# Agent attention and a feed-forward layer: where the query probabilities are split into two float32r parts

## The chip, the cores and the metric

The kernel runs on one core of a Trainium2 chip. The metric is the device time of one launch in microseconds; the kernel before took 1161.85 us, the median of three runs (1158.37 to 1161.86).

## The reference

Two layers follow each other. With q, k, v of shape (2, 12480, 128) and 49 agent vectors per batch:

```python
a2k = sm(agents, k)        # softmax over 12480 keys
agent_v = a2k @ v
q2a = sm(q, agents)        # softmax over 49 agents, one row per query
x = q2a @ agent_v
h = x @ w_in               # 128 -> 2048
g = where(h > 0, h, exp(min(h, 0)) - 1)
out = g @ w_out            # 2048 -> 128
```

All is float32 (the weights arrive as float64 and are converted on the chip).

## The kernel before, in words

The product `agent_v @ w_in` is formed once per batch as the table A (49 rows, 2048 columns), so that h is the query probabilities times A. A query block has 960 queries; there are 26 (13 for each batch). One block runs through 16 steps of the main loop: two halves of 480 query columns, eight steps each, and each step covers 256 of the 2048 hidden columns. A step s does, in this order: the score-side products `p1` (L397 to L406) into one of three PSUM tiles `h` of two banks, the output products `p2` of step s - 4 (L426 to L450) into two PSUM banks `o0` and `o1` that are held for eight steps, the activation `elu` (ACT Relu and Exp, L411 and L414, then DVE's combination into `g`, L416), and `split` (DVE casts half of `g` to `hi`, L422; GpSimd subtracts to get `lo`). When a half of a block ends, both output banks are evicted: `ob` by DVE (L442) and `oa` by ACT between its Relu and Exp (L446); GpSimd adds the two, and the next half's `p2` can write into the banks.

Products of float32 accuracy are made of two float32r parts, high and low: A has `ahi` and `alo`, w_out has `w_hi` and `w_lo` for one half of the hidden columns, and the query probabilities have `px0`, `px1`. The other half of w_out is `w_f`, a plain float32 tile, against which plain float32 `g` is multiplied.

The query probabilities of block j are made while block j - 1 is computed. `manual_schedule` keeps the order in which the program is written, and `at(s, fn, ...)` (L456) puts a piece of work behind step s; pieces at the same step stand in the order in which they were added. Scores, row maximum and subtraction come first; then the exponential on ACT (`q_exp`, one step on), the row sums and a small operation that adds 1e-9 (`q_sum`, `q_rz(0)`, L326), the reciprocal and the normalisation in place (`q_rz(1)`, `q_mul`, L333), the cast to the high part on ACT (`q_hi`, L338, a helper at L193), and the low part on DVE (`q_lo`, L342, a helper at L198). Their tiles `pp_hi` and `pp_lo` hold 120 queries in the partitions and four pairs of 49 probabilities in columns 0 to 48 and 64 to 112. `q_ring` (L362) takes one `h` tile, turns both parts with TensorE's transpose (L355, eight in all), has DVE copy each bank to `px` (L358), and sends `px` by DMA on SP's queue to `py` with the two halves of the partitions exchanged (L359, L360).

Block 0 is made in a prologue (L459 to L606), which also takes the key statistics of batch 0, and in which weight chunks are converted by DVE, ACT and GpSimd. `plan` (L560 on) lists its order row by row, and rows 8 to 22 have extra matmuls `busy(6)` behind them that only occupy TensorE. While the first half of the main loop runs, the key scores of batch 1 are computed in it as well (two rounds per block, `k_round`); in the middle, its weighted sums (`ev1`).

Of the kernel before, what the change touches and what calls it, by code (L numbers as in the profile page):

```python
# [8 lines left out]
F32 = mybir.dt.float32  # L9
F32R = mybir.dt.float32r  # L10
I32 = mybir.dt.int32
U32 = mybir.dt.uint32
ACTF = mybir.ActivationFunctionType
ALU = mybir.AluOpType
AX = mybir.AxisListType

TP = 120
R = 8
# [4 lines left out]
def tile_agent_attention_moe(  # L23
# [10 lines left out]
    nc = tc.nc  # L34
    B, C, N = kT.shape
    NA = agT.shape[2]
    ROWS = (0, 64)
    NA2 = ROWS[1] + NA
# [3 lines left out]
    T = G // 2  # L42
# [11 lines left out]
    const = ctx.enter_context(tc.tile_pool(name="const", bufs=1))  # L54
# [4 lines left out]
    sm_p = ctx.enter_context(tc.tile_pool(name="sm", bufs=2))  # L59
# [2 lines left out]

    ag_sb = const.tile([C, B, NA], F32)
    ident = const.tile([128, 128], F32)
    ident_r = const.tile([128, 128], F32R)
    dup = const.tile([NA, NA2], F32)
    ones = const.tile([NA, TP], F32)
    pp_hi = const.tile([TP, R // 2, NA2], F32R)
    pp_lo = const.tile([TP, R // 2, NA2], F32R)
    win_sb = big.tile([C, DFF], F32)  # L70
    w_f = big.tile([128, NP, 128], F32)
    w_hi = big.tile([128, NP, 128], F32R)
# [38 lines left out]
    k_t, v_t, q_t, p_t, A = {}, {}, {}, {}, {}  # L111
# [17 lines left out]
    idle = []  # L129
    held = {}  # L130

    def slot(dt=F32):

        return ps_h.tile([128, 2, 512], dt, tag="h", name="h")
# [36 lines left out]
    def k_max_t(run, ps):  # L171
        nc.tensor.transpose(ps[:NA, :TP], run, ident[:TP, :TP])
        mx_st["pt"] = ps

    def k_max_d(g):
        nc.vector.tensor_reduce(out=mcs[:, g:g + 1], in_=mx_st["pt"][:NA, :TP], axis=AX.X, op=ALU.max)
        attn_free(mx_st.pop("pt"))
        dg = sm_p.tile([NA, NA], F32, tag="dg", name="dg")
        nc.vector.tensor_scalar(out=dg, in0=ident[:NA, :NA], scalar1=mcs[:, g:g + 1], scalar2=None, op0=ALU.mult)
        mx_st["dg"] = dg  # L180
# [10 lines left out]
    def cast_hi(eng, out, x):  # L191
        if eng is nc.scalar:
            nc.scalar.activation(out=out, in_=x, func=ACTF.Copy)  # L193
        else:
            eng.tensor_scalar(out=out, in0=x, scalar1=1.0, scalar2=0.0, op0=ALU.mult, op1=ALU.add)

    def rest(eng, out, x, hi):
        eng.tensor_tensor(out=out, in0=x, in1=hi.bitcast(F32), op=ALU.subtract)  # L198
# [94 lines left out]
    q_st = {}  # L293
# [29 lines left out]
    def q_rz(half):  # L323
        z = q_st["z"]
        if half == 0:
            nc.vector.tensor_scalar(out=z, in0=z, scalar1=1e-9, scalar2=None, op0=ALU.add)  # L326
        else:
            q_st["z"] = sm_p.tile([TP, R], F32, tag="z", name="z")
            nc.vector.reciprocal(out=q_st["z"], in_=z)

    def q_mul(eng):
        e = q_st["e"]
        eng.tensor_tensor(out=e, in0=e, in1=q_st["z"].unsqueeze(2).to_broadcast([TP, R, NA]), op=ALU.mult)  # L333

    def halves(t):
        return [t[:, :, r:r + NA] for r in ROWS]

    def q_hi(eng):  # L338
        for h, t in enumerate(halves(pp_hi)):
            cast_hi(eng, t, q_st["e"][:, h * (R // 2):(h + 1) * (R // 2), :])  # L340

    def q_lo(eng, lo=0, hi=R):  # L342
        for x in range(lo, hi, R // 2):
            h = x // (R // 2)
            rest(eng, halves(pp_lo)[h], q_st["e"][:, x:x + R // 2, :], halves(pp_hi)[h])

    def q_tr(j, banks):

        p_t[j] = []
        for part, (src, ps) in enumerate(zip((pp_hi, pp_lo), banks)):  # L350
            x = sm_p.tile([NA2, T], F32R, tag=f"px{part}", name=f"px{part}")
            y = sm_p.tile([NA2, T], F32R, tag=f"py{part}", name=f"py{part}")
            p_t[j].append((x, y))
            for i in range(R // 2):
                nc.tensor.transpose(ps[:NA2, i * TP:(i + 1) * TP], src[:, i, :], ident_r[:TP, :TP])  # L355
        a, b = [slice(r, r + NA) for r in ROWS]
        for (x, y), ps in zip(p_t[j], banks):
            nc.vector.tensor_copy(out=x, in_=ps[:NA2, 0:T])  # L358
            nc.sync.dma_start(out=y[a].bitcast(F32), in_=x[b].bitcast(F32))  # L359
            nc.sync.dma_start(out=y[b].bitcast(F32), in_=x[a].bitcast(F32))  # L360

    def q_ring(j):  # L362
        t = slot(F32R)
        q_tr(j, [t[:, i, :] for i in range(2)])

    wr_t = {}

# [5 lines left out]
    def wo_step(c):  # L373

        if c not in wo_gen:
            even = wc_p.tile([128, 2, 128], F32, tag="even", name="even")
            w_e[c] = even
            pick = [lambda x, i=i: x.rearrange("p (m i d) -> p m i d", i=2, d=128)[:, :, i, :] for i in range(2)]
            wo_gen[c] = f64_steps(wr_t.pop(c), [(even, pick[0]), (w_f[:, 2 * c:2 * c + 2, :], pick[1])])
        next(wo_gen[c])  # L380
# [71 lines left out]
    act, dve, pool = nc.scalar, nc.vector, nc.gpsimd  # L452
# [3 lines left out]
    def at(s, fn, *a):  # L456
        pre.setdefault(s, []).append((fn, a))

    with tc.manual_schedule():  # L459
        with tc.tile_pool(name="pro", bufs=5) as pro, tc.tile_pool(name="ps_p", bufs=1, space=bass.MemoryType.PSUM) as ps_p:  # L460
# [5 lines left out]
            def win_step(c):  # L466
                if c not in win_gen:
                    win_gen[c] = f64_steps(win_r.pop(c), [(win_sb[:, c * 512:(c + 1) * 512], lambda x: x)])
                next(win_gen[c])
# [33 lines left out]
            dve.memset(ones, 1.0)  # L503
            dve.memset(s_all[:, :, R:R + 1, :], 0.0)
            dve.memset(ebias, -8.0 * 896 * 2 ** 20)
            dve.tensor_copy(out=ident_r, in_=ident)
            dve.memset(dup, 0.0)
            dve.memset(pp_hi.bitcast(F32), 0.0)
            dve.memset(pp_lo.bitcast(F32), 0.0)
            for r in ROWS:  # L510
                dve.tensor_copy(out=dup[:, r:r + NA], in_=ident[:NA, 0:NA])
            hk = ps_p.tile([128, 2, 512], F32, tag="hk", name="hk")
# [21 lines left out]
            for c, t in enumerate(CONV):  # L534
                f = [lambda c=c: win_step(c) if c < 4 else wo_step(c - 4)] * 7
                f = [f[0:2], f[2:4], f[4:6], f[6:7]]
# [5 lines left out]
            def conv():  # L542
                for x in ff.pop(0):
                    x()

            qq = [q_max, q_sub, q_exp, q_sum, lambda: q_rz(0), lambda: q_rz(1), lambda: q_mul(dve), lambda: q_hi(act), lambda: q_lo(dve)]

            def run(l, n=1):
                for _ in range(n):
                    l.pop(0)()  # L550

            def top(g):
                k_max_t(runs[g], hk[:, 0, :])
                k_max_d(g)

            def spread():
# [15 lines left out]
                ("s11", "p7", lambda: run(qq, 2)),  # L572
                ("e4", lambda: run(qq, 2)),
                ("s12", "p8", lambda: run(qq, 2)),
                ("e5", lambda: run(qq, 3)),
                (lambda: top(2), lambda: q_tr(0, [x.bitcast(F32R) for x in idle]), ev0_scale),
                ("e6", spread, "p9"),
                ("e7", "p10"),
                ("e8", "p11"),
# [39 lines left out]
        for j in range(1, B * NG):  # L619
            s0 = (j - 1) * NM + EDGE  # L620
            if j + 1 < B * NG:
                at(s0 + 1, load_q, j + 1)
            if j > 1:
                s0 -= NP
            at(s0 - 2 * (j == 1), q_scores, j, 0, R)
            at(s0 - 2 * (j == 1), q_max)
            at(s0 - 2 * (j == 1), q_sub)
            at(s0 + 1, q_exp)
            at(s0 + 2, q_sum)
            at(s0 + 2, q_rz, 0)  # L630
            at(s0 + 3, q_rz, 1)
            at(s0 + 3, q_mul, dve)
            at(s0 + 4, q_hi, act)
            at(s0 + 5, q_lo, dve, 0, 4)
            at(s0 + 6, q_lo, dve, 4, 8)
            at(s0 + (9 if j == 1 else NP + 4), q_ring, j)
        def k_round(r):
            ps = attn_bank()
# [3 lines left out]
        for r in range(NR):  # L642
            s0 = (r // 2) * NM + 13 + 4 * (r % 2)
# [8 lines left out]
        for r in range(NR):  # L652
            s0 = (7 + r // 3) * NM + 8 + 4 * (r % 3)
# [57 lines left out]
```

## Time and profile before

| | |
|---|---|
| median of three runs | 1161.85 us |
| lowest and highest run | 1158.37 and 1161.86 us |
| span of the profiled execution, first to last instruction | 1156.0 us |
| TensorE busy | 1122.3 us, 97% of the span |
| ACT busy | 898.3 us, 78% |
| DVE busy | 875.5 us, 76% |
| GpSimd busy | 599.8 us, 52% |
| 16 DMA engines | 58 GB/s on average |

The page gives the profiled execution's span and no other time of its own. A busy TensorE is not TensorE at its peak: matmuls are pipelined and their ends are modelled, so the time that one takes is best read from the start of one group to the start of the next. In the table, time in which an engine waits for a semaphore is not busy.

### The profile page before, as it was taken

Reading aid. Unit: us, or ns where it says so; the run is one execution under the profiler, and the core shown is the slowest. Engines: PE = TensorE matmul, PEld = TensorE weight load, DVE = VectorE, ACT = ScalarE, POOL = GpSimd, SP = SyncE. Lnnn points to the kernel's source line nnn. Section 1 sums busy time; section 2 is a strip of 40 time slices with the busy share of each in tenths; the row PEclk is TensorE's granted clock in tenths of the full one; section 3 lists DMA queues with packets and bytes.
Section 4 is the critical chain, followed back from the end, with each engine's and each line's share of the span. In section 5 each row is a group of like instructions: output and inputs, shape, how many; then the busy total and the mean of one; then the engine's idle time right before and its main releaser. Section 6 shows DMA issues by size and latency. Waiting matters only on the chain.

```text
span 1156.0 us, 21922 instructions
## 1 busy us (share of the span) xinstructions
PE 1122.3 (97%) x8364; PEld 871.2 (75%) x8364; DVE 875.5 (76%) x1313; ACT 898.3 (78%) x1050; POOL 599.8 (52%) x495
## 2 busy tenths in 40 slices
PE   9987999999999999999999999999999999999998
PEld 9974777777777777777776777777777777777787
DVE  5538777777777877777778877887788778877875
ACT  3217788788888878778778888888888888888896
POOL 0114555455555545545545555555555565655565
PEclk9999999999999999999999999999999999999999
DMA  9940121121121221221101101110111011101000
GB/s 297 256 139 1 40 82 44 40 82 56 33 77 57 69 74 57 69 75 57 35 24 40 35 23 49 39 35 23 48 40 35 23 48 37 38 23 48 19 23 18
DMA packets 25711, 66.66 MB, mean 58 GB/s; under 512 B 3054, under 2 KB 14806, under 8 KB 25606
## 3 DMA queue, kind: packets, MB, share of 16 engines
q1 hardware_dynamic: 25606, 65.26, 18.6%
q8 instruction: 66, 1.08, 0.4%
q14 instruction: 39, 0.32, 0.1%
HBM read 42.68 MB, written 12.78 MB: 48 GB/s over the span
## 4 chain that ended last, share of the span: by engine, by line
PE 76%; DVE 9%; ACT 4%; issue 2%; POOL 0%; DVEq 0%; POOLq 0%; ACTq 0%
PE o L437 45%; PE h L405 21%; PE h L150 6%; DVE g L416 6%; ACT e L411 2%; PE h L211 2%; PE h L355 2%; ACT e L414 1%; DVE hi L422 1%; DVE pp_lo L198 1%; DVE ob L442 1%; ACT pp_hi L193 1%; DVE qe L333 1%; PE h L264 0%; DVEq L422 0%
## 5 line engine op out<-in xcount | busy, mean ns | idle before, releaser
L198 POOL TENSOR_TENSOR lo<-g,hi 128x480 fp32r<-128x480 f32 x416 | 521.3, 1253 | 495.1 <-DVE hi L422 394.9
L416 DVE SCALAR_TENSOR_TENSOR g<-e,h 128x960 f32<-128x960 f32 x416 | 479.5, 1153 | 171.0 <-ACT e L414 168.5
L411 ACT ACTIVATE e<-h 128x960 f32<-128x960 f32 x416 | 401.6, 965 | 115.9 <-PE h L405 99.6
L414 ACT ACTIVATE e<-e 128x960 f32<-128x960 f32 x416 | 418.4, 1006 | 11.6
L437 PE MATMUL o<-g,w_f 64*128 64x480 f32 x1664 | 427.4, 562 | 0.0
L437 PE MATMUL o<-lo,w_hi 64*128 64x480 f32 x832 | 338.0, 751 | 0.0
L405 PE MATMUL h<-px,ahi 49*128 49x480 f32 x832 | 259.0, 391 | 4.6 <-DVE alo L286 3.9
L405 PE MATMUL h<-py,ahi 49*128 49x480 f32 x832 | 258.9, 391 | 0.5 <-DVE g L416 0.5
L422 DVE CAST hi<-g 128x480 fp32r<-128x480 f32 x416 | 179.5, 431 | 54.6 <-PE o L437 2.0
L437 PE MATMUL o<-hi,w_lo 64*128 64x480 f32 x832 | 189.4, 384 | 16.5 <-ACT oa L446 7.1
L437 PEld LDWEIGHTS o<-g,w_f 64*128 64x128 f32 x1664 | 181.7, 185 | 19.6
L437 PE MATMUL o<-hi,w_hi 64*128 64x480 f32 x832 | 184.4, 380 | 0.0
L405 PEld LDWEIGHTS h<-px,ahi 49*128 49x128 f32 x832 | 149.0, 187 | 41.0 <-issue 22.1
L405 PEld LDWEIGHTS h<-py,ahi 49*128 49x128 f32 x832 | 149.0, 187 | 38.3 <-issue 24.9
L405 PE MATMUL h<-py,alo 49*128 49x480 f32 x416 | 157.1, 378 | 0.0
L405 PE MATMUL h<-px,alo 49*128 49x480 f32 x416 | 157.0, 377 | 0.0
L437 PEld LDWEIGHTS o<-lo,w_hi 64*128 64x128 f32 x832 | 101.0, 186 | 67.1 <-issue 58.0
L437 PEld LDWEIGHTS o<-hi,w_lo 64*128 64x128 f32 x832 | 100.2, 185 | 41.2 <-ACT oa L446 17.3
L437 PEld LDWEIGHTS o<-hi,w_hi 64*128 64x128 f32 x832 | 99.2, 187 | 9.3
L405 PEld LDWEIGHTS h<-py,alo 49*128 49x128 f32 x416 | 77.0, 185 | 5.9
L405 PEld LDWEIGHTS h<-px,alo 49*128 49x128 f32 x416 | 77.1, 185 | 4.1
L447 POOL TENSOR_TENSOR ob<-ob,oa 128x480 f32<-128x480 f32 x52 | 63.3, 1217 | 3.9 <-ACT oa L446 3.9
(125 smaller groups left out, 794.7 us busy)
## 6 DMA issues: line engine op xcount, KB each, us to landing
v<-in_vx_dram SPq DMA_DIRECT2D x26, 483.8 KB
k<-in_kT_dram SPq DMA_DIRECT2D x26, 480.0 KB
q<-in_qT_dram SPq DMA_DIRECT2D x26, 480.0 KB
out_dram<-ob SPq DMA_DIRECT2D x52, 240.0 KB
py<-px SPq DMA_DIRECT2D x104, 91.9 KB
raw<-in_w_out_dram SPq DMA_DIRECT2D x4, 512.0 KB
raw<-in_w_in_dram SPq DMA_DIRECT2D x3, 512.0 KB
k<-in_w_in_dram SPq DMA_DIRECT2D x1, 512.0 KB
```

The source lines that it names most:

```text
L150: nc.tensor.matmul(out=ps[:TP, j * NA:(j + 1) * NA], lhsT=src[:, j * TP:(j + 1) * TP], rhs=ag_sb[:, b, :], start=True, stop=True)
L193: nc.scalar.activation(out=out, in_=x, func=ACTF.Copy)
L198: eng.tensor_tensor(out=out, in0=x, in1=hi.bitcast(F32), op=ALU.subtract)
L211: nc.tensor.matmul(out=ps, lhsT=s_all[:, r, j:j + 2, :].rearrange("p t a -> p (t a)"), rhs=v_t[b, r][:, j, :], start=(r == rs[0] and j == ...
L355: nc.tensor.transpose(ps[:NA2, i * TP:(i + 1) * TP], src[:, i, :], ident_r[:TP, :TP])
L405: nc.tensor.matmul(out=h[:, u, 0:T], lhsT=a[x, :], rhs=p[u ^ half][x, :], start=i == 0, stop=i == 2)
L411: nc.scalar.activation(out=e, in_=h, func=ACTF.Relu, scale=-1.0)
L414: nc.scalar.activation(out=e, in_=e, func=ACTF.Exp, scale=-1.0)
L416: nc.vector.scalar_tensor_tensor(out=g, in0=e, scalar=-1.0, in1=h, op0=ALU.add, op1=ALU.max)
L422: nc.vector.tensor_copy(out=hi_t[s], in_=g_t[s][:, 0, :])
L437: nc.tensor.matmul(out=o_t[u][:, 0:T], lhsT=w[x, c, :], rhs=v[x, :], start=first and i == 0, stop=last and i == len(jobs) - 1)
L447: nc.gpsimd.tensor_tensor(out=ob, in0=ob, in1=oa, op=ALU.add)
```

## The change

The normalisation writes its product to one float32 tile `pp` in place of `e`, and there is no split in front of the transposes. Four float32 transposes write to one bank; ACT copies the bank to the high part `px0` (rounding to float32r), and DVE subtracts this from the bank to get the low part `px1`. The exchanges by DMA stand behind each part as before. `q_mul` stands one step later than it did, and `q_hi` and `q_lo` with their places at steps 4, 5 and 6 are gone.

```diff
-    ident_r = const.tile([128, 128], F32R)
-    pp_hi = const.tile([TP, R // 2, NA2], F32R)
-    pp_lo = const.tile([TP, R // 2, NA2], F32R)
+    pp = const.tile([TP, R // 2, 128], F32)
...
+    def q_mul():
+        e = q_st["e"].rearrange("p (h i) a -> p h i a", h=2)
+        z = q_st["z"].rearrange("p (h i) -> p h i", h=2).unsqueeze(3).to_broadcast([TP, 2, R // 2, NA])
+        out = pp.rearrange("p i (h a) -> p h i a", h=2)[:, :, :, 0:NA]
+        nc.vector.tensor_tensor(out=out, in0=e, in1=z, op=ALU.mult)
+
+    def q_tr(ps):
+        for i in range(R // 2):
+            nc.tensor.transpose(ps[:NA2, i * TP:(i + 1) * TP], pp[:, i, 0:NA2], ident[:TP, :TP])
+        q_st["tr"] = ps[:NA2, 0:T]
+
+    def q_parts(j, part):
+        ps = q_st["tr"]
+        if part == 0:
+            p_t[j] = []
+        x = sm_p.tile([NA2, T], F32R, tag=f"px{part}", name=f"px{part}")
+        y = sm_p.tile([NA2, T], F32R, tag=f"py{part}", name=f"py{part}")
+        p_t[j].append((x, y))
+        if part == 0:
+            nc.scalar.activation(out=x, in_=ps, func=ACTF.Copy)
+        else:
+            rest(nc.vector, x, q_st.pop("tr"), p_t[j][0][0])
         a, b = [slice(r, r + NA) for r in ROWS]
+        nc.sync.dma_start(out=y[a].bitcast(F32), in_=x[b].bitcast(F32))
+        nc.sync.dma_start(out=y[b].bitcast(F32), in_=x[a].bitcast(F32))
...
     def q_ring(j):
-        t = slot(F32R)
-        q_tr(j, [t[:, i, :] for i in range(2)])
+        q_tr(slot()[:, 0, :])
+        q_parts(j, 0)
+        q_parts(j, 1)
...
-            dve.tensor_copy(out=ident_r, in_=ident)
-            dve.memset(pp_hi.bitcast(F32), 0.0)
-            dve.memset(pp_lo.bitcast(F32), 0.0)
+            dve.memset(pp, 0.0)
...
-                ("e5", lambda: run(qq, 3)),
-                (lambda: top(2), lambda: q_tr(0, [x.bitcast(F32R) for x in idle]), ev0_scale),
+                ("e5", lambda: run(qq, 1)),
+                (lambda: top(2), lambda: q_tr(idle[0]), lambda: q_parts(0, 0), lambda: q_parts(0, 1), ev0_scale),
...
             at(s0 + 3, q_rz, 1)
-            at(s0 + 3, q_mul, dve)
-            at(s0 + 4, q_hi, act)
-            at(s0 + 5, q_lo, dve, 0, 4)
-            at(s0 + 6, q_lo, dve, 4, 8)
+            at(s0 + 4, q_mul)
             at(s0 + (9 if j == 1 else NP + 4), q_ring, j)
```

## Rows read from the trace of the kernel before

**Rows 1.** Busy time by stretch: length, then each engine's busy us (instructions), clock, DMA

```profile
200.00:400.00 200.00, 199.49 (x1503) 152.89 (x1500) 158.33 (x236) 164.46 (x189) 106.95 (x88) 1.00 0.19 57
800.00:1000.00 200.00, 194.52 (x1448) 146.20 (x1446) 160.15 (x228) 168.15 (x192) 114.91 (x93) 1.00 0.11 35
```

**Rows 2.** Waits of TensorE, 620 to 1156 us: total us, times, longest

```profile
PE o L437 <- ACT oa L446: 7.1, 12, 0.6
PE o L437 <- DVE ob L442: 6.0, 12, 0.5
```

**Rows 3.** Timeline at one such wait: start, us, engine, line, operation, [idle before, releaser]

```profile
725.60 0.63 ACT L193 ACTIVATE pp_hi<-qe 120x196 fp32r<-120x196 f32 x2 [1.42 <-DVE qe L333]
...
731.87 0.38 PE L405 MATMUL h<-px,ahi 49*128 49x480 f32 x1
...
732.68 0.56 ACT L446 ACTIVATE oa<-o 128x480 f32<-128x480 f32 x1
...
733.29 0.48 PE L437 MATMUL o<-hi,w_lo 64*128 64x480 f32 x1 [0.60 <-ACT oa L446]
...
735.62 0.38 PE L405 MATMUL h<-px,ahi 49*128 49x480 f32 x1
```

**Rows 4.** Timeline, the same step of an earlier pass and the step before it

```profile
187.30 0.38 PE L405 MATMUL h<-py,ahi 49*128 49x480 f32 x1
...
188.17 0.39 PE L437 MATMUL o<-hi,w_hi 64*128 64x480 f32 x2
...
188.39 0.97 PE L437 MATMUL o<-g,w_f 64*128 64x480 f32 x4
...
188.82 0.76 PE L437 MATMUL o<-lo,w_hi 64*128 64x480 f32 x2
...
189.41 0.38 PE L405 MATMUL h<-px,ahi 49*128 49x480 f32 x1
...
191.79 0.38 PE L405 MATMUL h<-px,ahi 49*128 49x480 f32 x1
```

**Rows 5.** Timeline of TensorE at the eight transposes of block 1

```profile
128.11 0.61 PE L355 MATMUL h<-ident_r,pp_hi 120*113 120x120 f32 x4
128.55 0.56 PE L355 MATMUL h<-ident_r,pp_lo 120*113 120x120 f32 x4
129.04 0.49 PE L405 MATMUL h<-py,ahi 49*128 49x480 f32 x1
```

**Rows 6.** Line 172: count, duration ns minimum/median/maximum, first and last start

```profile
L172 PE MATMUL hk<-ident,mrun x3: 268/268/268, 17.3 to 59.3; 120*49 120x120 f32 x3
```

**Rows 7.** Line 355, in the same columns

```profile
L355 PE MATMUL h<-ident_r,pp_hi x100: 261/264/313, 128.1 to 1091.9; 120*113 120x120 f32 x100
```

**Rows 8.** Groups by line: count, busy us, mean ns, idle before and releasers

```profile
L414 ACT ACTIVATE e<-e 128x960 f32<-128x960 f32 x416 | 418.4, 1006 | 11.6
L411 ACT ACTIVATE e<-h 128x960 f32<-128x960 f32 x416 | 401.6, 965 | 115.9 <-PE h L405 99.6 <-DVE g L416 1.4
...
L358 DVE CAST px<-h 113x480 fp32r<-113x480 f32 x50 | 30.4, 650 | 0.0
L446 ACT ACTIVATE oa<-o 128x480 f32<-128x480 f32 x52 | 29.5, 568 | 23.1 <-PE o L437 23.1
...
L326 DVE TENSOR_SCALAR z<-z 120x8 f32<-120x8 f32 x26 | 22.1, 850 | 0.9
L198 DVE TENSOR_TENSOR pp_lo<-qe,pp_hi 120x196 fp32r<-120x196 f32 x52 | 18.9, 366 | 0.4 <-ACT pp_hi L193 0.4
```

**Rows 9.** Timeline of TensorE at the transposes of block 0 in the prologue

```profile
60.65 0.61 PE L355 MATMUL at<-ident_r,pp_hi 120*113 120x120 f32 x4 [1.10 <-ACT pp_hi L193]
...
61.56 0.61 PE L355 MATMUL at<-ident_r,pp_lo 120*113 120x120 f32 x4 [0.30 <-DVE pp_lo L198]
```

**Rows 10.** Busy time by stretch around the end of the prologue

```profile
62.00:80.00 18.00, 18.00 (x161) 17.80 (x161) 5.41 (x13) 2.26 (x5) 1.26 (x1) 1.00 0.49 163
80.00:120.00 40.00, 29.25 (x159) 18.32 (x159) 29.88 (x48) 26.82 (x37) 17.10 (x17) 0.87 0.00 1
```

More of the change, by code (lines that the diff above doesn't have):

```diff
@@ L329, in q_rz @@
             nc.vector.reciprocal(out=q_st["z"], in_=z)
[L331 to L355, printed above, removed]
+    def q_mul():
[3 more added lines that the diff above has]
+        nc.vector.tensor_tensor(out=out, in0=e, in1=z, op=ALU.mult)
@@ L356, in q_tr @@
         a, b = [slice(r, r + NA) for r in ROWS]
[L357 to L360, printed above, removed]
+        nc.sync.dma_start(out=y[a].bitcast(F32), in_=x[b].bitcast(F32))
+        nc.sync.dma_start(out=y[b].bitcast(F32), in_=x[a].bitcast(F32))
     def q_ring(j):
-        t = slot(F32R)
@@ L544, in conv @@
                     x()
-            qq = [q_max, q_sub, q_exp, q_sum, lambda: q_rz(0), lambda: q_rz(1), lambda: q_mul(dve), lambda: q_hi(act), lambda: q_lo(dve)]
+            qq = [q_max, q_sub, q_exp, q_sum, lambda: q_rz(0), lambda: q_rz(1), q_mul]
             def run(l, n=1):
```

## The prediction

> **What bounds the kernel now.** I read the busy time of the engines by stretch first, then the list of who waited for whom on TensorE alone, then the timeline around the places that list names. In the table by stretch the reader is to see that TensorE is busy 199.49 of 200 us in the first stretch and 194.52 of 200 in the second, at a granted clock of 1.00 in both, while DVE, ACT and POOL are well below [rows 1]. So from about 130 us on every TensorE instruction that goes is time saved, and work taken from DVE or ACT is worth only what TensorE waits for them. The wait list says what that is: in the second half 7.1 us in 12 waits for ACT's eviction `oa` and 6.0 us in 12 for DVE's eviction `ob` [rows 2].
>
> The timeline shows why. ACT sits 1.42 us before it can cast `pp_hi`, because DVE's normalisation of the probabilities comes late; the pair of casts starts at 725.60 and takes 0.63 us. The Relu, the two Exps and the evictions behind it are late, `oa` among them (732.68), and the first matmul into the output bank waits 0.60 us for it [rows 3]. From the first score matmul of that step (731.87) to that of the next (735.62) are 3.75 us; the same step of an earlier pass, where ACT is on time, takes 191.79 - 189.41 = 2.38 us, and an ordinary one 189.41 - 187.30 = 2.11 us [rows 3, 4]. The late eviction thus costs 1.37 us, more than the idle time that the list shows, in each of 12 passes. In the first half key scores give TensorE other work before that step, and the stretch there has no such idle time [rows 1].
>
> **The change part by part.** One query block has 8 transposes before (4 for the high part, 4 for the low) and 4 after. Blocks 1 to 25 do this in the main loop, block 0 in the prologue.
>
> *Transposes.* Four float32r transposes start at 128.11, the next four at 128.55, the next matmul at 129.04: 0.44 and 0.49 us for four, 0.93 us for eight [rows 5]. What a float32 transpose of 113 columns costs is not in the trace; the nearest is the float32 transpose of the running maximum, 120x49 against a 120-column identity: one instruction a call and 268 ns, against a median of 264 ns for the float32r ones [rows 6, 7]. I take the same price, so four go for nothing in return: 25 x 0.46 = 11.5 us. The dear end: float32 products with `w_f` take two instructions each, where the float32r ones take one, and from their first to the next step are 189.41 - 188.39 = 1.02 us, of which the two `lo` matmuls are some 0.22 (as 188.17 to 188.39), leaving 0.80 against 0.22, 3.6 times [rows 4]. At that price four transposes would cost 4 x 0.116 x 3.6 = 1.67 us, 0.74 more than the eight now, or +18.5 us in 25 blocks. The cheap end is the 11.5 gained, since nothing in the rows makes a float32 transpose cheaper than a float32r one. I stay with the row that is itself a transpose.
>
> The Trainium skill ("FP8 and Floating Point Precision", section TensorE Precision Notes) states that true FP32 takes four passes through the array; by it the four transposes would cost 4 x 4 x 0.116 = 1.86 us, about +23 us in all. Its page "TensorE: Matmul & The Clock Gate" (section Terms) says that the transpose mode is four times faster for FP32, which would cancel that; the trace agrees with the first for the products (3.6 times) and with the second for the only float32 transpose it has (one instruction, 268 ns).
>
> *ACT.* The two casts go, 0.63 us for the pair [rows 3], and with them the wait for the normalisation. One copy of 113x480 from PSUM comes, at the place of the transposes; nearest is the 128x480 eviction, 568 ns [rows 8]. It waits for the four transposes, and behind it are the next step's Relu and Exp, for which DVE waits. ACT needs 0.965 + 1.006 = 1.97 us for a step's two functions [rows 8] against 2.11 for TensorE, so it has 0.14 to spare; but in the step with the transposes TensorE itself needs 0.46 more. 0.57 - 0.46 - 0.14 is about zero, and two steps would clear a tenth. The transposes stand on TensorE right behind the output matmuls of that step, while ACT is still in its Exp, so I count no wait: 0. If that cover goes, it is the second rival.
>
> *DVE.* Two subtractions of 366 ns and two casts of 650 ns go; one subtraction of 113x480 out of PSUM comes, for which I take the 650 ns of the cast of that size [rows 8], between nothing and twice that. That is 1.4 us less per block, on an engine that TensorE doesn't wait for except at `ob`. The subtraction waits for ACT's copy, and the next step's g is behind it; both are due before that step's Exp ends. Its bank comes free after copy and subtraction, 1.2 us, as after the two casts now (1.3), and the next user is three steps on. The normalisation moves one step later and writes a strided tile; it still stands five steps or more ahead of its transposes, and nothing on ACT waits for it any more.
>
> *The stall.* With the casts, ACT loses the 1.42 + 0.63 us that made `oa` late four steps on. What is late next: DVE's g, by the small operation on the sums (850 ns [rows 8]) and what stands with it; DVE is busy 160.15 of 200 us [rows 1], so it has 0.4 us of a 2.11 us step to spare and is back within the five steps to that eviction. So I count the on-time step: 12 x 1.37 = 16.4 us, between 0 and that.
>
> *Transfers.* The four exchanges of halves per block are issued as now, in SP's order; the first pair waits for ACT instead of DVE, at about the same time, and their readers come nine steps later (four in the first block): 0. The loads behind them on SP keep their place.
>
> *Prologue.* TensorE waits 1.10 us for `pp_hi` and 0.30 for `pp_lo`, with four transposes between [rows 9]. With the second four gone and no split ahead of the first, the prologue's matmuls move up by about 1.5 us (60.65 + 0.91 + 0.45 now, about 60.5 then), and from there TensorE is busy 18.00 of 18.00 us, so the shift reaches the main loop [rows 10]. Behind it, from 80 to 120 us, the clock is at 0.87 on average, that is, in the lower of its two levels (1.2 instead of 2.4 GHz) in some stretches, after TensorE had waited; where they fall may shift, for which I allow 2 us either way. Two memsets and a copy of the identity at the start stand beside the first loads: 0.
>
> Sum: 11.5 + 16.4 + 1.5 = 29.4 us off the profiled span of 1156.0. The page gives the span alone; the median of the runs, 1161.85, is 5.85 above it, and I let that stay: about 1133 us.
>
> **The rivals.** *One: the stall stays.* DVE is late by then for its own reasons (that small operation, and the normalisation now a step later) and `ob`, not `oa`, holds the bank. For it: both are in the wait list [rows 2]. Against: `ob` stands behind a chain that starts with ACT's late Relu [rows 3]. Only transposes and prologue then: 1161.85 - 13 = 1149 us.
>
> *Two, the other side: ACT's new copy makes the next eviction late.* ACT is in order, and the copy holds Relu and Exp until the transposes are done. If wait and copy come to more than ACT's slack up to the next output eviction, four steps on (4 x 0.14 + 0.46 = 1.0 us), `oa` is late there, and TensorE pays 1.37 us in up to 25 blocks, 34 us against the 29 gained: about 1167 us. For it: this is the mechanism of [rows 3], and ACT has little slack. Against: the copy itself is 0.57, so the wait would have to be over 0.45 us, while TensorE's order has the transposes done before the Exp ends; and query scores stand ahead of that eviction's readers.
>
> *Three: float32 transposes cost what float32 products cost.* With the 3.6 times above and the stall gone: 1161.85 + 18.5 - 16.4 - 1.5 = 1162.5 us, no change. By the four passes of the Trainium skill ("FP8 and Floating Point Precision", TensorE Precision Notes) it would be a little dearer, about 1167 us.
>
> *Four: the change doesn't shorten TensorE's work:* a float32 transpose takes twice a float32r one (two instructions, as the products have). Stall and prologue remain: 1161.85 - 18 = 1144 us. Against it: the count in [rows 6].
>
> **How the numbers follow.** Forecast 0.60, one 0.16, four 0.09, three 0.06, two 0.06, the rest 0.03 (spread over both signs). A difference under 0.3%, 3.5 us, cannot be told from none in this kernel. Forecast, one and four are faster: 0.85, and a little of the rest; three is the same, 0.06; two and some of the rest slower, 0.08. The range starts at 1125: the forecast less 2 us for the clock's places, 2 for a second half that also gains in DVE's waits, and 3.5 for the medians; it ends at 1151, past rivals one and four: 0.85 or a little less inside.
>
> **What would show it.** Right: 104 transposes instead of 208, some 265 ns each, blocks' next score matmul 0.45 us after the first transpose; no ACT wait for the normalisation; no waits of TensorE for `oa` and `ob` in the second half, or of a tenth or two; the copy from PSUM with no wait above 0.2 us. Wrong: transposes in two instructions or far above 300 ns; a new wait of ACT for them with a late `oa` four steps on; `ob` waits that stay; a passage from prologue to main loop that keeps its place.

## The result and the profile after

The changed kernel took 1136.43 us (median of four runs, 1133.41 to 1138.15), the kernel before 1161.86 beside it: a ratio of 0.9762, 95% interval 0.9726 to 0.9798. The profiled span went from 1156.0 to 1131.6 us, 24.4 less. In the line of the page with the busy times of the engines (share of the span, instructions), TensorE is busier in share and less in sum:

```profile
PE 1111.7 (98%) x8260; PEld 865.9 (77%) x8260; DVE 838.7 (74%) x1233; ACT 903.7 (80%) x1024; POOL 593.5 (52%) x495
```

The table by stretch, for the kernel after (columns as in [rows 1]):

```profile
200.00:400.00 200.00, 199.95 (x1498) 152.20 (x1498) 155.72 (x223) 166.53 (x186) 107.54 (x89) 1.00 0.19 58
800.00:1000.00 200.00, 199.99 (x1490) 153.78 (x1488) 157.57 (x220) 179.30 (x196) 119.28 (x98) 1.00 0.13 41
```

In the second half TensorE now has no gap, 199.99 of 200 us against 194.52. ACT is busier there (179.30 against 168.15 us) though it has less to do for each block: it does more blocks in the same time and waits less. A list of TensorE's waits from 610 us on, which had 24 entries for `oa` and `ob` [rows 2], is empty.

The timeline at the step that answers to [rows 3]: DVE's normalisation is done 5 us before the eviction and nothing on ACT waits for it, and the eviction waits only for its own matmuls:

```profile
719.87 0.56 DVE L333 TENSOR_TENSOR pp<-qe,z 120x392 f32<-120x392 f32 x1
...
725.30 0.38 PE L399 MATMUL h<-px,ahi 49*128 49x480 f32 x1
...
725.50 0.57 ACT L440 ACTIVATE oa<-o 128x480 f32<-128x480 f32 x1 [0.47 <-PE o L431]
...
726.12 0.67 PE L431 MATMUL o<-hi,w_lo 64*128 64x480 f32 x2
...
727.69 0.39 PE L399 MATMUL h<-px,ahi 49*128 49x480 f32 x1
```

From score matmul to score matmul it is 727.69 - 725.30 = 2.39 us, where it was 3.75 [rows 3] and 2.38 in a pass that was on time [rows 4].

The transposes of one block, and then line 337 and the two new evictions by group (columns as in [rows 5, 7, 8]):

```profile
199.56 0.67 PE L337 MATMUL h<-ident,pp 120*113 120x120 f32 x4
200.16 0.49 PE L399 MATMUL h<-py,ahi 49*128 49x480 f32 x1
```

```profile
L337 PE MATMUL h<-ident,pp x100: 266/266/358, 130.0 to 1068.3; 120*113 120x120 f32 x100
```

```profile
L196 DVE TENSOR_TENSOR px<-h,px 113x480 fp32r<-113x480 f32 x25 | 16.3, 651 | 0.0
...
L348 ACT ACTIVATE px<-h 113x480 fp32r<-113x480 f32 x25 | 14.2, 569 | 0.9
```

One instruction a transpose, 266 ns in the median, four in 0.60 us to the next matmul against 0.93 for eight [rows 5]. ACT's copy takes 569 ns and hardly waits (0.9 us in 25), DVE's subtraction 651.

Where the 24.4 us are, by the first transpose of each block (60.65, 128.11, 624.60 and 1091.54 us before; 63.79, 129.99, 621.85 and 1067.90 after):

| stretch | before | after | difference | forecast |
|---|---|---|---|---|
| start to block 0 | 60.65 | 63.79 | +3.1 | 0 |
| block 0 to block 1 | 67.46 | 66.20 | -1.3 | -1.5 |
| block 1 to block 13 | 496.49 | 491.86 | -4.6 | 12 x 0.46 = -5.5 |
| block 13 to block 25 | 466.94 | 446.05 | -20.9 | 12 x 1.83 = -22.0 |
| block 25 to the end | 64.46 | 63.70 | -0.8 | -0.5 |

The first two rows are of one trace each and vary from run to run: the changed kernel, measured again below, has 65.12 and 68.69 us there. The two rows of the main loop repeat (491.89 and 446.08 us).

One block of the second half, first in the kernel before, then in the one after (38.77 and 37.07 us). This period, from two rows, is what the experiments below are read by; the last eleven of the half lie between 38.77 and 38.83 us before and between 37.06 and 37.08 after:

```profile
703.47 0.61 PE L355 MATMUL h<-ident_r,pp_hi 120*113 120x120 f32 x4
...
742.24 0.61 PE L355 MATMUL h<-ident_r,pp_hi 120*113 120x120 f32 x4
```

```profile
697.23 0.67 PE L337 MATMUL h<-ident,pp 120*113 120x120 f32 x4
...
734.30 0.67 PE L337 MATMUL h<-ident,pp 120*113 120x120 f32 x4
```

The only stretch that became longer is the start. TensorE waits longer for the first query block (before, then after):

```profile
43.89 1.88 PE L150 MATMUL at<-ag_sb,q 128*120 128x49 f32 x16 [1.17 <-DMA q<-in_qT_dram]
```

```profile
46.04 1.88 PE L148 MATMUL at<-ag_sb,q 128*120 128x49 f32 x16 [3.13 <-DMA q<-in_qT_dram]
```

### The profile page after: what moved, and what is told of

Read it like the earlier page. It is cut to its first block, busy times and chain, and to the rows that moved or that the text cites. A ratio compares the mean times of both kernels' runs of the same rounds, so it can differ in the third digit from the quotient of the medians.

```text
span 1131.6 us, 21624 instructions
## 1 busy us (share of the span) xinstructions
PE 1111.7 (98%) x8260; PEld 865.9 (77%) x8260; DVE 838.7 (74%) x1233; ACT 903.7 (80%) x1024; POOL 593.5 (52%) x495
## 4 chain that ended last, share of the span: by engine, by line
PE 89%; DVE 2%; ACT 1%; issue 1%; POOL 0%; POOLq 0%; DVEq 0%; ACTq 0%
PE o L431 54%; PE h L399 25%; PE h L148 6%; PE h L209 2%; PE h L337 1%; DVE g L410 1%; PE h L262 1%; ACT e L408 0%; ACT e L405 0%; DVE ex L101 0%; DVE fr L103 0%; DVE fr L95 0%; POOLq L696 0%; DVE hi L416 0%; POOL lo L196 0%
## 5 line engine op out<-in xcount | busy, mean ns | idle before, releaser
L196 POOL TENSOR_TENSOR lo<-g,hi 128x480 fp32r<-128x480 f32 x416 | 515.0, 1238 | 474.1 <-DVE hi L416 397.5
L416 DVE CAST hi<-g 128x480 fp32r<-128x480 f32 x416 | 172.3, 414 | 53.4 <-PE o L431 0.5
L431 PE MATMUL o<-hi,w_lo 64*128 64x480 f32 x832 | 182.9, 384 | 3.3 <-POOL w_lo L196 3.3
L431 PE MATMUL o<-hi,w_hi 64*128 64x480 f32 x832 | 179.7, 377 | 0.0
```

Source lines behind the costliest of these rows:

```text
L416: nc.vector.tensor_copy(out=hi_t[s], in_=g_t[s][:, 0, :])
L431: nc.tensor.matmul(out=o_t[u][:, 0:T], lhsT=w[x, c, :], rhs=v[x, :], start=first and i == 0, stop=last and i == len(jobs) - 1)
```

## The experiments

The theory: ACT, which works in order, was late by a wait and two casts, and through its evictions made TensorE wait in the second half; transposes are the rest. The rival: DVE's lighter load made the difference. In the diffs, `d` and the like are for blocks 2 to 25; block 1 keeps its order.

**Undoing ACT's relief in the changed kernel.**

```diff
-            at(s0 + 4, q_mul)
+            at(s0 + (3 if j > 1 else 4), q_mul)
+            if j > 1:
+                at(s0 + 4, q_dummy, 196)    # two ACT copies of pp, 120x196 each
```

> The changed kernel, with the normalisation back at its old step and two casts of 120x196 on ACT at the old place whose result nobody reads; four float32 transposes and the light DVE work stay. Theory (ACT alone makes the eviction late): the waits for oa and ob come back, 12 x 1.37 = 16.4 us more than the changed kernel, 1150 to 1154 us. Rival (the relief of DVE): no more than 4 us above the changed kernel's 1136.

1150.17 us (1148.53 to 1153.09), ratio to the kernel before 0.990 (0.9877 to 0.9922). TensorE's waits in the second half, and the period:

```profile
PE o L436 <- ACT oa L445: 6.9, 12, 0.6
PE o L436 <- DVE ob L441: 6.0, 12, 0.5
```

```profile
702.77 0.67 PE L337 MATMUL h<-ident,pp 120*113 120x120 f32 x4
...
741.25 0.67 PE L337 MATMUL h<-ident,pp 120*113 120x120 f32 x4
```

All 24 waits are back and the period is 38.48 us, 1.41 above the changed kernel's. DVE is as light as in the changed kernel, and `ob` is late all the same: it stands behind a `g` that ACT makes late. So the loss needs none of the DVE work that went; with the 0.36 us of four more transposes, 38.48 gives 38.84, about the period of the kernel before (38.77 to 38.83). This run and the next one also bring the normalisation back a step earlier on DVE. That place alone doesn't make `oa` late: three runs of the kernel before, further below, keep it, take ACT's wait away and have no wait for `oa` in the second half.

**Wait and work apart.** Two more edits of the changed kernel at the same place: first the wait without the casts (one column copied from the normalised tile), then the casts without the wait (they read the exponentials, and the normalisation keeps its new step).

```diff
-            at(s0 + 4, q_mul)
+            at(s0 + (3 if j > 1 else 4), q_mul)
+            if j > 1:
+                at(s0 + 4, q_dummy)         # one ACT copy of pp[:, 0, 0:1]
```

> The changed kernel with the normalisation back at its old step and, at the old place of the casts, one ACT copy of a single column of its result: ACT waits for the normalisation as before, but casts nothing. By the run with the casts one step later (period in the second half 37.89 us, 0.46 above the 37.43 that eight transposes would leave without a stall), the wait is worth 0.9 of the 1.4 us: period 37.9 to 38.1 us against 37.07, 10 to 12 us above the changed kernel. If the casts alone make it: period 37.1 to 37.2, the changed kernel's time.

```diff
+            if j > 1:
+                at(s0 + 4, q_dummy)         # two ACT copies of e, 120x196 each
             at(s0 + 4, q_mul)
```

> The changed kernel with two ACT copies of 120x196 at the old place of the casts that read the exponentials, which ACT itself made three steps before: 0.63 us of work and no wait. If wait and work add up, period 37.5 to 37.6 us, 5 to 6 us above the changed kernel. If only the wait counts: 37.1 us, no difference.

The wait alone: 1147.09 us (1142.41 to 1151.39), with these waits and this period:

```profile
PE o L435 <- DVE ob L440: 6.0, 12, 0.5
PE o L435 <- ACT oa L444: 1.0, 6, 0.2
```

```profile
702.46 0.67 PE L337 MATMUL h<-ident,pp 120*113 120x120 f32 x4
...
740.56 0.67 PE L337 MATMUL h<-ident,pp 120*113 120x120 f32 x4
```

The casts alone: 1138.93 us (1136.59 to 1139.52), no waits, and

```profile
700.09 0.67 PE L337 MATMUL h<-ident,pp 120*113 120x120 f32 x4
...
737.20 0.67 PE L337 MATMUL h<-ident,pp 120*113 120x120 f32 x4
```

The periods are 38.10 and 37.11 us against 37.07: the wait (with its copy of 0.20 us) costs 1.03 us a block, the casts 0.04, both together 1.41. They don't add up (I had expected 0.5 for the casts). The casts alone fit into ACT's slack: ACT still idles 0.47 us ahead of `oa`, as in the changed kernel. In the two runs with the wait ACT's gaps between the wait and `oa` are under 0.05 us; there the slack is used up, and the casts cost 0.4 more.

**Moving the split in the kernel before,** all its work kept.

```diff
+            d = 5 if j > 1 else 0
-            at(s0 + 4, q_hi, act)
-            at(s0 + 5, q_lo, dve, 0, 4)
-            at(s0 + 6, q_lo, dve, 4, 8)
+            at(s0 + 4 + d, q_hi, act)
+            at(s0 + 5 + d, q_lo, dve, 0, 4)
+            at(s0 + 6 + d, q_lo, dve, 4, 8)
```

> The kernel before, with the cast and the two subtractions of the split five steps later (behind the output eviction that was late, still ahead of the transposes); all instructions stay, eight transposes too. Theory (ACT waits for the normalisation and casts, so Relu, Exp and oa behind it are late): the 12 + 12 waits of TensorE for oa and ob in the second half go, 12 x 1.37 = 16.4 us less, about 1145 us. Rival (the saving in the second half comes from the DVE work that the change took away): that work is still there, so ob stays late and the time is within 4 us of 1162.

1160.26 us (1153.86 to 1166.36), ratio 0.9984 (0.996 to 1.0009): missed. The time is the one that the rival gave, but not in the rival's way: the waits for `oa` and `ob` are gone. Instead the transposes wait for the subtraction just ahead of them, 5.5 us in 11 waits in the first half and 2.6 us in 11 in the second:

```profile
PE h L355 <- DVE pp_lo L198: 5.5, 11, 0.8
```

With both subtractions one step behind the cast (the second at `s0 + 10`):

> As the run with the split behind the eviction, but both subtractions one step behind the cast, so that the transposes two steps on need not wait for them (the earlier run traded the lost stall for waits of TensorE for pp_lo, 8 us in all). All work of the kernel before stays. Theory (ACT's wait and casts make oa late): no waits for oa, ob or pp_lo in the main loop, period of a block in the second half 38.81 - 1.38 = 37.43 us, 16 us less than before, 1144 to 1148 us. Rival (the DVE work that went): 1156 us or more.

1158.36 us (1154.09 to 1161.64), ratio 0.9978 (0.9959 to 0.9998): missed again, with a time that was the rival's. The waits from 130 to 610 us, and the longest from 610 us on (the other two are 0.8 us in all):

```profile
PE h L405 <- DVE g L416: 4.5, 11, 0.5
```

```profile
PE h L405 <- DVE g L416: 3.5, 12, 0.5
```

No wait for `oa`, `ob` or `pp_lo` is left, and a block of the second half takes 709.74 to 747.59, 37.85 us, 0.9 less than before. But the casts now stand behind the eviction, where ACT has just spent 0.57 us on `oa`, and TensorE's score matmuls wait for `g` instead, in both halves: from block 1 to block 13 are 502.87 us where the kernel before has 496.49. With the cast moved by one step only (`d = 1`):

> The kernel before, with cast and subtractions one step later: the normalisation is long done when ACT reaches the cast, so the wait of 1.4 us goes, while the 0.63 us of casting still stands four steps ahead of the eviction. If the wait makes oa late: most of the 16.4 us goes, 1146 to 1150 us, with TensorE waits for oa under 0.3 us each. If the casting itself does it: over half of the loss stays, 1155 us or more.

1154.32 us (1152.56 to 1156.74), ratio 0.9935 (0.991 to 0.9961), between the two times expected; the period is 746.39 - 708.54 = 37.85 us as well. No wait for `oa` is left, and those for `ob` fall to 2.5 us in 12. The timeline shows where they come from:

```profile
737.14 0.57 ACT L446 ACTIVATE oa<-o 128x480 f32<-128x480 f32 x1 [0.47 <-PE o L437]
...
737.43 0.35 DVE L198 TENSOR_TENSOR pp_lo<-qe,pp_hi 120x196 fp32r<-120x196 f32 x1
...
737.71 0.65 DVE L442 COPY ob<-o 128x480 f32<-128x480 f32 x1
```

ACT is on time, casts and all: it idles 0.47 us ahead of `oa`, as in the changed kernel. But the edit has moved DVE's second subtraction to the place right ahead of `ob`. That step takes 739.76 - 736.94 = 2.82 us where the changed kernel's takes 2.39, and these 0.43 us are what the period has above the 37.4 that eight transposes without a stall would leave (37.07 + 0.36). So in the kernel before, too, ACT is late by the wait and not by the casts alone, and the rest of the loss here is the subtraction's new place. The first half is 2.9 us longer in this run (499.34 us from block 1 to block 13). None of the three orders tried reaches 37.4 us.

**The price of a transpose.** Each transpose of the changed kernel twice:

```diff
         for i in range(R // 2):
+            for _ in range(2):
-            nc.tensor.transpose(...)
+                nc.tensor.transpose(...)
```

> The changed kernel, with each float32 transpose issued twice into the same place (eight a block). If a float32 transpose costs what a float32r one does (0.116 us): 25 x 0.46 = 11.5 us more, period of a block in the second half 37.07 + 0.46 = 37.53 us. If it is dearer, as the saving of 0.36 to 0.39 us a block in the first half hints (0.93 - 0.37 = 0.56 for four, 0.14 each): 14 us more, period 37.63 us. If it costs two float32r ones: 23 us more, period 38.0 us.

1143.82 us (1141.35 to 1146.86), a group of eight and the next matmul:

```profile
203.59 1.07 PE L338 MATMUL h<-ident,pp 120*113 120x120 f32 x8
204.60 0.48 PE L400 MATMUL h<-py,ahi 49*128 49x480 f32 x1
```

Eight take 1.01 us and four 0.60, so a further one costs 0.10 us, and a group has some 0.2 us beside that. The period is 743.61 - 706.14 = 37.47 us, 0.40 above the changed kernel's; I had expected 0.46 to 0.56. Then four float32r ones, with tile and identity in float32r:

> The changed kernel with its tile and identity in float32r: four float32r transposes in place of four float32 ones (the low part then holds next to nothing, since the tile is rounded when it is written). The changed kernel's four take 0.60 us to the next matmul, the first 0.19 of it. If the price is the data type's: 0.44 to 0.48 us and a period of 36.93 us; if a group of four simply has that fixed part: 0.60 us and 37.07 us.

One run, 1137.64 us:

```profile
203.13 0.61 PE L338 MATMUL h<-ident_r,pp 120*113 120x120 f32 x4
203.67 0.48 PE L400 MATMUL h<-py,ahi 49*128 49x480 f32 x1
```

0.54 us against 0.60, between the two that I had expected: nine tenths of the price is that of any group of four; float32 adds 0.06 us to a group here, and 0.08 to a group of eight (1.01 against 0.93). The period in the second half is 37.02 to 37.06 us, up to 0.05 under the changed kernel's.

**The start.** In the three variants of the kernel before, the first query block's scores begin at 43.76, 44.12 and 45.25 us (1.7 to 1.8 us of waiting); in the variants of the changed kernel with an unchanged load order, at 45.16 to 46.89 (2.9 to 3.5 us). I asked whether the changed kernel repeats it, whether the addresses of the tiles do it, and whether an earlier load ends it.

> The changed kernel as it is, once more beside the next two. If the late landing of the first query block (46.04 against 43.89 us) was chance, it lands at 44 here; if it belongs to this program, at 46 to 46.6 again, as in the two variants of it measured so far. Time 1133 to 1139 us.

> The changed kernel with an unused tile of 2080 bytes a partition behind the constants, so that all tiles behind them (loads of keys and values too) lie at the addresses that they have in the kernel before. If the address of the loads' targets makes the values land later in the prologue: the first query block lands at about 44 us, TensorE's wait for it falls from 3.1 to under 2 us, and the time falls by 1 to 3 us. If not, no difference over 1 us and the block lands at 46 again.

```diff
+    pad = const.tile([128, 520], F32)
...
+            dve.memset(pad[:, 0:1], 0.0)
```

> The changed kernel with the first query block's load issued ahead of one value, one key and one weight load (no other edit). It then lands some 5 us earlier, TensorE does not wait for it (3.1 us now), and the clock has no cause to fall behind that wait: 2 to 5 us less than the changed kernel in the same call, unless a load that now comes later (a value block at 50 us, a weight chunk) makes TensorE wait in its place, in which case nothing changes.

```diff
-            dma = {..., 7: "v3 k11 v4 k12 o0 q0 v5", ...}
+            dma = {..., 7: "v3 k11 q0 v4 k12 o0 v5", ...}
```

The changed kernel again took 1135.33 us (1134.28 to 1137.31), the one with the old addresses 1132.29 (1129.51 to 1138.6), the one with the early load 1131.09 (1128.47 to 1134.97). The first matmul of the query scores in the first two:

```profile
45.75 2.64 PE L148 MATMUL at<-ag_sb,q 128*120 128x49 f32 x13 [3.48 <-DMA q<-in_qT_dram]
```

```profile
45.70 2.64 PE L149 MATMUL at<-ag_sb,q 128*120 128x49 f32 x12 [3.25 <-DMA q<-in_qT_dram]
```

The long wait repeats, and the addresses are not its cause, whatever the 3 us between the medians are (the runs' ranges overlap). With the early load that wait is gone, and TensorE waits 2.4 us for the normalised tile of block 0 in its place:

```profile
PE at L337 <- DVE pp L333: 2.4, 1, 2.4
```

The granted clock from 40 to 60 us is 1.00, where the changed kernel measured beside it has 0.83; this is what I had expected. The median with the early load is 4.2 us under that kernel's; against the kernel before the ratios are 0.9742 (0.9714 to 0.977) and 0.9779 (0.9753 to 0.9805), intervals that just overlap. It has the lowest median of all kernels measured here, but the 4.2 us can't be put down to the load by the medians: the kernel with the old addresses has 3.0 of them with the wait in place.

## Why the prediction was right, and where its sizes were off

*The bound and the stall: right.* TensorE fills the main loop, and the second half's wait came from ACT's order. Four fewer transposes account for 0.36 us of a block's 1.70 (the saving between blocks 1 and 13, where there was no such wait: 41.43 - 41.07); 1.34 are left for the stall, for which I had 1.37. The time alone would not have shown it, since the range took in rivals one and four as well; the empty wait list and the edits of ACT's order do. Putting ACT's burden back costs 1.41. What I had not seen is that the wait is the cause and the casts only matter behind it (1.03, 0.04, 1.41 together).

*The transposes: the term that was mis-sized.* I halved the 0.93 us and took 0.46; it is 0.33 by the timeline of a group and 0.36 to 0.39 by the blocks, 9 us in all instead of 11.5. The next score matmul, which I had 0.45 us behind the first transpose, comes after 0.60. The step from one group of four to the next (0.44) was read as the price of four, but a group has a fixed part that four transposes pay as eight do. The direction of the choice between float32's two prices was right: one instruction, 266 ns, and 0.06 us more than float32r for a group. Rival three (the price of float32 products) and rival four (two instructions) are refuted by the count and by this. The four passes that the Trainium skill gives for FP32 ("FP8 and Floating Point Precision", TensorE Precision Notes) do not hold for these transposes: four float32 ones take 0.60 us, float32r ones 0.54. What the Trainium skill says of the transpose mode ("TensorE: Matmul & The Clock Gate", Terms) agrees with the trace.

*ACT's copy and DVE's subtraction: right.* 569 and 651 ns, for which I had 568 and 650, and 0.9 us of ACT's waiting in 25 blocks. Rival two needed 0.45 us of waiting in each and did not come. Rival one, that the stall stays because DVE makes `ob` late, did not come either: no wait for `ob` is left.

*The prologue: right in itself, covered by something else.* Block 0's transposes wait 0.46 us instead of the 1.10 of [rows 9], and from the first of them to the next other matmul pass 0.50 us instead of 62.01 - 60.65 = 1.36 (before, then after):

```profile
62.01 1.56 PE L499 MATMUL two<-warm 128*128 128x128 f32 x12
```

```profile
63.79 0.67 PE L337 MATMUL at<-ident,pp 120*113 120x120 f32 x4 [0.46 <-DVE pp L333]
64.29 1.51 PE L493 MATMUL two<-warm 128*128 128x128 f32 x12
```

That is 0.64 + 0.86 = 1.50 us, the 1.5 of the prediction. The table's -1.3 from block 0 to block 1 is not this term, and lies near the forecast by chance: the first part lies ahead of that stretch, and the changed kernel again needed 68.69 us for it, more than the 67.46 before.

The start, for which I had nothing, is 3.1 us longer even so. The scores of the first query block begin 2.15 us later (46.04 against 43.89), and behind the longer wait TensorE has a lower granted clock, 0.64 on average instead of 1.00, so in part the lower of its two levels (before, then after, columns as in [rows 1]):

```profile
47.70:52.40 4.70, 4.70 (x45) 4.70 (x45) 3.92 (x9) 1.96 (x5) 2.69 (x4) 1.00 0.98 204
```

```profile
47.70:52.40 4.70, 4.70 (x31) 4.70 (x30) 2.10 (x4) 2.08 (x4) 1.73 (x3) 0.64 0.98 236
```

The work from these scores to the last matmul ahead of block 0's transposes takes 17.03 us instead of 15.39, 1.64 more; with the 2.15 and less the 0.64 this is the 3.1. It is 18.65 us in the changed kernel again and 15.30 with the early load, but 18.65 in two variants of the kernel before as well, so that a part of the start is the run's and not the change's. Why the block lands later in the changed kernel is open: the load order is the same, and the addresses of the tiles are excluded. In this pair of traces its load is also issued later (30.02 us against 29.13), but it was issued at 28.71 in the changed kernel again, with the same long wait. From its issue to the scores pass 14.6 to 14.9 us in the kernel before and its three variants, and 15.6 to 17.0 in the changed kernel and all its variants with the same load order.

So 29.4 us forecast and 24.4 measured in the span differ by 5.0 us: by the table, 3.1 at the start, 0.2 between block 0 and block 1 and 1.7 behind that, where the transposes are the term that was too large. The medians fell by 25.4 us, to 1136.43; the sum of the prediction gives 1161.85 - 29.4 = 1132.45, which it rounds to 1133.

## What to carry to other kernels

On an engine that works in order, ask of each small instruction whom it waits for and what queues behind it: a wait of 1.4 us on ACT cost TensorE 1.0 us a block, four steps later and under the name of an eviction, while the same casts without a wait cost 0.04. Moving such a piece is not free either: each of three other places turned a part of the gain, or all of it, into a wait for something else. Read a prologue from several runs: its length varied by some 4 us between two runs of one kernel. Take the price of one more instruction from groups of two sizes, not from the average of one group.

## What the runs showed of the hardware that was not expected

A further float32 transpose of 120x113 costs 0.10 us in a group, as a float32r one does, and the group some 0.2 us beside them (float32r 0.15). The first transpose of a float32 group is longer in the records (358 ns against 266) than the first of a float32r group (313 against 263). ACT's wait and its work did not add up: 1.03 and 0.04 us apart, 1.41 together.
